# Moving two sums of the second half of a seven-product tile behind the first bank's reads

## The chip, the cores and the metric

The kernel runs on one core of one Trainium2 chip. The time is that of one execution on the device in microseconds (us). The kernel before takes 839.22 us, the median of three runs (838.73 to 839.88). The profile shows one further execution.

## The reference

The input x holds 8 batches of 3008 rows of 256 values. A mixing layer works along the rows, and a layer of two matrix products with a squared ReLU follows:

```
X  = rfft(x, axis=1)                     # per batch, along the 3008 rows
Yr = X.real @ w_r - X.imag @ w_i + b_r   # 256 x 256
Yi = X.real @ w_i + X.imag @ w_r + b_i
Yr, Yi = soft threshold of both at 0.01
y  = irfft(Yr + 1j*Yi, n=3008, axis=1)   # 24064 rows of 256 in all

h   = y @ w_in                           # 256 -> 2048
r   = max(h, 0)
g   = s * r*r + b                        # s and b are scalars
out = g @ w_out                          # 2048 -> 256
```

## The kernel before, in words

**The Fourier layer** is done as small matrix products with constant tables (94 times 32 points). In the steady part it is cut into units (the functions `s1_units`, `s23_units` and `s4_units`), each of a few matmuls into one PSUM bank of the pool `psf` (two banks) and an evacuation by ScalarE (ACT, L187) or VectorE (DVE, L189). Intermediate results go through DRAM (`ud`, `vd`) and come back by transfers on SP's queue, such as `us<-ud` (L644, 384 KB each, four a batch).

**The two matrix products** run over tiles of up to 512 rows. The main loop (L1134 to L1146) takes tile `ti` through 16 slots. In each slot it issues the units of the Fourier layer that the plan puts there, then one sixteenth of the first product of tile `ti` (`first_mm`: two matmuls of 512 columns into `psh`), then one sixteenth of the second product of tile `ti - 1`. After each second slot ACT takes the ReLU out of `psh` (L871, `rt`), and the square into `gt` is taken by ACT (L881) or by DVE (L884). Which one is decided while the program is written down: the function `work` adds an assumed cost to an engine's load, and `act_first` compares the two loads at that point. So an operation that stands elsewhere in the program moves other squares and evacuations between ACT and DVE.

**Seven products instead of eight.** For 21 tiles of 480 or 512 rows (`seven`, L1073: among the last two tiles ahead of each batch's first tile, the first tile of batches 1 and 3 to 6, and those of the last batch but its end) the second product is taken as a 2 by 2 block product with seven block multiplications, n = 0 to 6 in `seven_mms`. The activations of a tile have four blocks a11, a12, a21, a22, each in two halves q = 0 and q = 1 (hidden units 0 to 1023 and 1024 to 2047). `s_op(ti, n, q)` makes the sums that the products need:

- sum 1: s1 = a21 + a22, on DVE, read by product 3
- sum 3: a21 = a11 - a21, on DVE, read by product 5
- sum 2: a11 = a11 - s1, on DVE, after sums 1 and 3 and after product 0 has read a11; read by product 4
- sum 4: a12 = a12 + a11, an accumulating DMA on POOL's queue (L973), after sum 2 and after product 1 has read a12; read by product 6

The products share PSUM banks: {0, 1}, {2}, {3, 4} and {5, 6}. Outside the last batch these banks come from the pool `psa`, which has two buffers. So product 3 opens its bank only when the bank of products 0 and 1 has been read. The reads are `leave(group)`: group 0 reads products 0 and 1 on DVE (L1028 into `zz`, L1029 into `ost`; both run through the helper's line L1012), followed by L1030, which needs no bank. Groups 1, 2 and 3 read the other banks. In the last batch (`alone`) the banks come from both pools, there is no Fourier work left, and product 2 is taken together with products 0 and 1.

The 112 matmuls of the seven products are spread seven to a slot (L1059). In a slot the sums come after its matmuls, and then the reads. The framework then schedules the program: each engine has one queue, in which an instruction that waits holds up all behind it, and the order within a queue can differ from that of the program text, so that a sum, a square and a read may change places. `tc.issue_after(x)` binds the instructions of its block to stand behind x on x's engine.

Of the kernel before, what the change touches and what calls it, by code (L numbers as in the profile page):

```python
# [11 lines left out]
ALU = mybir.AluOpType  # L12
# [84 lines left out]
def kernel(  # L97
# [13 lines left out]
    nc = tc.nc  # L111
    B, S, D = x.shape
# [4 lines left out]
    MC = DFF // P  # L117
# [3 lines left out]
    first, fwd, inv, last = _tables(N)  # L121
# [50 lines left out]
    def matmul(out, lhs, rhs, **how):  # L172
        if pe["on"]:
            pe["now"] += 0.0025 + int(np.prod(rhs.shape[1:])) / 2400.0
        return nc.tensor.matmul(out, lhs, rhs, **how)  # L175

    def work(engine, us):
        load[engine] = max(load[engine], pe["now"]) + us
# [32 lines left out]
    def sum_bank(ti):  # L211
        return any_bank() if ti >= mark[B - 1] // MC else other_bank()
# [149 lines left out]
    b_21 = cpool.tile([P, P], F32, name="b_21")  # L362
# [3 lines left out]
    def w_block(k, j):  # L366
        return w_out_t.rearrange("p (q k) d -> p q k d", k=2)[:, :, k, j * P : (j + 1) * P]
# [447 lines left out]
    def sub_size(tl):  # L815
        return 4 * tl[3] if tl[0] == "wide" else P
# [69 lines left out]
    def store(tl, sub, src):  # L886
        kind, b, j, w = tl
        if kind == "wide":
            h, lo = j
            n2 = HW * h + 4 * sub  # L890
            rows = out[b * N : (b + 1) * N, :].rearrange("(n1 n2) d -> n2 n1 d", n2=N2)
            nc.sync.dma_start(
                out=rows[n2 : n2 + 4, lo : lo + w], in_=src[0 : 4 * w]
            )
            return
        if kind == "main":
            rows = out[b * N + 512 * j : b * N + 512 * (j + 1), :]
            rows = rows.rearrange("(n1 n2) d -> n2 n1 d", n2=N2)[8 * sub : 8 * sub + 8]
            nc.sync.dma_start(out=rows, in_=src)
            return  # L900
        i0 = j + 128 * sub
        end = min(i0 + 128, j + w)
        i = i0
        while i < end:
            hb, r = divmod(i, N2 * 14)
            n2, n1 = divmod(r, 14)
            bt = 2 * b + hb
            rows = out[bt * N + 80 * N2 : (bt + 1) * N, :].rearrange(
                "(n1 n2) d -> n2 n1 d", n2=N2
            )  # L910
            room = min(end, (hb + 1) * N2 * 14) - i
            if n1 == 0 and room >= 14:
                m = room // 14
                cnt = 14 * m
                dst = rows[n2 : n2 + m]
            else:
                cnt = min(14 - n1, room)
                dst = rows[n2, n1 : n1 + cnt]
            nc.sync.dma_start(out=dst, in_=src[i - i0 : i - i0 + cnt])
            i += cnt  # L920
# [40 lines left out]
    def part(ti, q, i, k):  # L961
        size = 2 * sub_size(tiles[ti])
        return gts[(ti, q)][:, i, k, :, 0:size]

    def s_op(ti, n, q):

        size = 2 * sub_size(tiles[ti])
        if n == 1:
            sums[(ti, q)] = spool.tile([P, 4, 2 * P], F16, name="s1", tag="s1")
        s1 = sums[(ti, q)][:, :, 0:size]  # L970
        a11, a12, a21, a22 = (part(ti, q, i, k) for i in range(2) for k in range(2))
        if n == 4:
            nc.gpsimd.dma_start(out=a12, in_=a11, accum_op=ALU.add)  # L973
            return
        out, a, b, op = {
            1: (s1, a21, a22, ALU.add),
            3: (a21, a11, a21, ALU.subtract),
            2: (a11, a11, s1, ALU.subtract),
        }[n]
        nc.vector.tensor_tensor(out=out, in0=a, in1=b, op=op)  # L980
        work("dve", 0.07 + size / 480.0)

    def seven_mms(ti):

        tl = tiles[ti]
        size = sub_size(tl)
        hold = {}
        left = [(0, 0), (0, 1), (1, 1), None, (0, 0), (1, 0), (0, 1)]
        firsts = (0, 2, 3, 5)
        T = T_s[0]  # L990
        right = [w_block(0, 0), w_block(1, 0), T[:, 3], T[:, 0], T[:, 1], T[:, 2], w_block(1, 1)]

        def mm(n, j, c):

            if n in firsts and j == 0 and c == 0:
                hold["ps"] = sum_bank(ti).rearrange("p (n j e) -> p n j e", n=2, j=2)
            if j == 0 and c == 0:
                hold[n] = hold["ps"][0:size, 0 if n in firsts else 1]
            q, g = divmod(c, 4)
            at = slice(j * size, (j + 1) * size)  # L1000
            if left[n] is None:
                lhs = sums[(ti, q)][:, g, at]
            else:
                lhs = gts[(ti, q)][:, left[n][0], left[n][1], g, at]
            matmul(
                hold[n][:, j], lhs, right[n][:, c],
                start=(n in firsts and j == 0 and c == 0), stop=(c == MC // 2 - 1),
                skip_group_check=True,
            )

        def add(out, of, other):
            nc.vector.scalar_tensor_tensor(  # L1012
                out=out, in0=of, scalar=s_bc[0:size], in1=other, op0=ALU.mult, op1=ALU.add
            )
            work("dve", 0.4)

        def wide(t):
            return t[0:size, 0:P].unsqueeze(1).to_broadcast([size, 2, P])

        def leave(group):  # L1020
            if group == 0:
                hold["z"] = zpool.tile([P, 2, 2, P], F32, name="zz", tag="zz")
            if group in (0, 3):
                hold["o", group] = opool.tile([P, 2, D], F32, name="ost", tag="ost")
            z = hold["z"][0:size]
            top = hold["o", 0][0:size]
            if group == 0:
                add(z[:, 0], hold[0], wide(bias_bc))  # L1028
                add(top[:, :, 0:P], hold[1], z[:, 0])  # L1029
                nc.vector.tensor_tensor(out=z[:, 1], in0=z[:, 0], in1=wide(b_21), op=ALU.add)  # L1030
                work("dve", 0.34)
            elif group == 1:
                add(z[:, 0], hold[2], z[:, 0])
            elif group == 2:
                add(z[:, 1], hold[3], z[:, 1])
                two = hold[4].rearrange("p j e -> p (j e)").unsqueeze(1).to_broadcast([size, 2, D])
                zs = z.rearrange("p h j e -> p h (j e)")
                add(zs, two, zs)
                work("dve", 0.27)
            else:  # L1040
                for h in range(2):
                    add(hold["o", 3][0:size, :, h * P : (h + 1) * P], hold[5], z[:, h])
                add(top[:, :, P:D], hold[6], z[:, 1])
                for i in range(2):
                    for j in range(2):
                        store(tl, 2 * (1 - i) + j, hold["o", 3 * (1 - i)][:, j, :])

        C = MC // 2
        alone = ti >= mark[B - 1] // MC
        early = 3 if alone else 2  # L1050
        order = [
            (n, j, c) for h in range(2) for n in range(early) for j in range(2)
            for c in range(4 * h, 4 * h + 4)
        ]
        order += [(n, j, c) for n in range(early, 6) for j in range(2) for c in range(C)]
        order += [(6, j, c) for h in range(2) for j in range(2) for c in range(4 * h, 4 * h + 4)]
        slots = [[] for _ in range(MC)]
        for at, what in enumerate(order):
            slots[at // 7].append(lambda w=what: mm(*w))  # L1059
        first = ((0, 1, 0), (1, 3, 0)) if late(ti) else ()  # L1060
        for at, n, q in (
            *first, (2, 2, 0), (2, 1, 1), (2, 4, 0), (3, 3, 1), (4, 2, 1), (5, 4, 1)
        ):
            at += alone and at > 3
            slots[at].append(lambda n=n, q=q: s_op(ti, n, q))
        for at, group in ((4 + alone, 0), (6, 1), (11, 2), (15, 3)):
            slots[at].append(lambda group=group: leave(group))
        return slots

    def late(ti):  # L1070
        return any(ti == mark[b] // MC for b in range(3, B - 1))
# [29 lines left out]
    mark = {}  # L1101
# [76 lines left out]
```

## Time and profile before

| what | value |
|---|---|
| median of three runs | 839.22 us |
| the profiled execution, its own time | 839.64 us |
| its span, first to last instruction | 837.9 us |
| granted TensorE clock, mean | 0.996 |
| PE (matmul) busy | 822.6 us, 98% |
| DVE busy | 706.9 us, 84% |
| ACT busy | 723.0 us, 86% |
| POOL busy | 86.2 us, 10% |

Some 1.7 us of the profiled execution lie outside its span, and it is 0.4 us above the median. PE's busy time is that of pipelined matmuls whose ends are modelled, so 98% says that matmuls follow one another nearly without a hole, and not that each hole is small: what PE loses shows as gaps between the starts of matmuls and in the list of waits.

### The profile page before, as it was taken

To read this page: it belongs to the slowest core of one execution; us is meant where nothing else is said; L and a number is where in the kernel's file an instruction comes from. 1 tells how busy PE (TensorE), PEld (TensorE's weight loads), DVE (VectorE), ACT (ScalarE), POOL (GpSimd) and SP (SyncE) were. 2 spreads that over 40 slices of the span, in tenths; PEclk is the share of its full clock that TensorE was granted. 3 is DMA by queue.
4 is the path that set the end of the run, shared out by engine and by line. 5 is a ranking of instruction groups with operands and counts; after the bars stand their busy time and mean duration, and the time that the engine had idled before them with its cause. 6 is when DMAs were issued, how large, how long until landed. Compare 5 with 4: busy or idle time off the path is not lost.

```text
span 837.9 us, 19547 instructions
## 1 busy us (share of the span) xinstructions
PE 822.6 (98%) x7662; PEld 600.7 (72%) x7662; DVE 706.9 (84%) x1104; ACT 723.0 (86%) x962; POOL 86.2 (10%) x114
## 2 busy tenths in 40 slices
PE   8999999999999999999999999999999999999997
PEld 7857767777677767777677676767767777767765
DVE  5888989978898888988889888797889988889885
ACT  4998988998899989998889988989889988788882
POOL 4540001100011001100011000100001000001000
PEclk8999999999999999999999999999999999999999
DMA  8954578345873378444773368723565333513321
GB/s 196 180 153 103 124 189 203 63 94 133 198 185 65 94 184 208 114 104 128 195 185 69 88 147 208 175 63 105 127 178 138 67 100 93 137 45 77 72 65 60
DMA packets 116670, 107.17 MB, mean 128 GB/s; under 512 B 12774, under 2 KB 100842, under 8 KB 115234
## 3 DMA queue, kind: packets, MB, share of 16 engines
q1 hardware_dynamic: 102498, 80.55, 33.6%
q0 software_dynamic: 14080, 25.37, 19.1%
q8 instruction: 60, 0.98, 0.5%
q14 instruction: 32, 0.26, 0.1%
HBM read 53.52 MB, written 46.66 MB: 120 GB/s over the span
## 4 chain that ended last, share of the span: by engine, by line
PE 75%; DVE 12%; ACT 6%; DMA 3%; issue 3%; SPq 0%; POOL 0%; DVEq 0%; POOLq 0%
PE psh L175 31%; PE psa L175 28%; PE psf L175 16%; ACT rt L871 3%; DVE gt L884 2%; DVE gt L980 2%; ACT gt L881 1%; DVE ring L699 1%; PE psm L175 1%; DMA gt<-gt 1%; DVE ost L1012 1%; DMA ring<-ring 1%; DVE s L980 1%; DMA x<-in_x_dram 1%; DVE zz L1012 1%
## 5 line engine op out<-in xcount | busy, mean ns | idle before, releaser
L871 ACT ACTIVATE rt<-psh 128x1024 f32<-128x1024 f32 (+2 forms) x384 | 386.7, 1008 | 57.0 <-PE psh L175 55.1
L175 PEld LDWEIGHTS <-gt 128*128 128x128 f16 (+1 forms) x3696 | 304.8, 101 | 167.7 <-DMA gt<-gt 0.5
L175 PE MATMUL psh<-yt,w_in 128*128 128x512 f16 (+1 forms) x1344 | 397.1, 378 | 0.1
L884 DVE TENSOR_TENSOR gt<-rt 128x1024 f16<-128x1024 f32 (+2 forms) x239 | 286.2, 1202 | 78.6 <-ACT rt L871 77.6
L175 PE MATMUL psa<-w_out_t,gt 128*128 128x256 f16 (+3 forms) x2448 | 310.9, 253 | 0.3 <-DMA gt<-gt 0.3
L175 PEld LDWEIGHTS <-w_in 128*128 128x128 f16 x1536 | 136.5, 98 | 24.4 <-issue 1.7
L881 ACT ACTIVATE gt<-rt 128x1024 f16<-128x1024 f32 (+2 forms) x145 | 150.8, 1040 | 3.4
L175 PE MATMUL psa<-T_s,gt 128*128 128x128 f16 (+1 forms) x944 | 79.4, 219 | 0.0
L973 POOL DMA_DIRECT2D gt<-gt x42 | 38.0, 905 | 316.2 <-PE psh L175 66.3
L187 ACT CAST u<-psf 96x512 f16<-96x512 f32 x96 | 55.6, 581 | 9.3 <-PE psf L175 8.6
L699 DVE TENSOR_TENSOR ring<-psf,s 128x512 f16<-128x512 f32 x84 | 57.7, 686 | 3.5 <-PE psf L175 2.5
L187 ACT CAST v<-psf 128x512 f16<-128x512 f32 x79 | 45.8, 583 | 13.6 <-PE psf L175 13.5
L234 POOL DMA_DIRECT2D x<-in_x_dram x36 | 19.2, 539 | 325.1 <-PE psf L175 324.0
L175 PE MATMUL psh<-tail,w_in 128*128 128x512 f16 (+1 forms) x192 | 52.1, 353 | 0.0
L175 PEld LDWEIGHTS <-xf 128*128 128x128 f16 x504 | 46.6, 98 | 6.6 <-DVE xf L672 1.5
L175 PE MATMUL psf<-W_g,xf 128*128 128x256 f16 x336 | 50.4, 272 | 0.0
L187 ACT CAST yt<-psf 128x470 f16<-128x470 f32 (+2 forms) x84 | 43.3, 534 | 3.4 <-PE psf L175 2.2
L1012 DVE SCALAR_TENSOR_TENSOR ost<-psa,s_bc,zz 128x256 f32<-128x256 f32 (+1 forms) x80 | 35.9, 480 | 9.8 <-PE psa L175 8.2
L187 ACT CAST xf<-psf 128x512 f16<-128x512 f32 x64 | 37.4, 585 | 4.2 <-PE psf L175 3.9
L945 DVE SCALAR_TENSOR_TENSOR ost<-psa,s_bc,bias_bc 128x512 f32<-128x512 f32 (+2 forms) x51 | 37.1, 727 | 3.8 <-PE psa L175 1.4
L175 PE MATMUL psf<-x,A_t 94*96 94x512 f16 x102 | 39.0, 382 | 1.4 <-ACT yt L187 0.3
L175 PE MATMUL psf<-C_t,vs 96*128 96x94 f16 (+1 forms) x484 | 37.9, 205 | 0.0
(118 smaller groups left out, 802.6 us busy)
## 6 DMA issues: line engine op xcount, KB each, us to landing
out_dram<-ost SPq DMA_DIRECT2D x152, 128.0 KB
ud<-u SPq DMA_DIRECT2D x56, 192.0 KB
us<-ud SPq DMA_DIRECT2D x28, 384.0 KB
vd<-v SPq DMA_DIRECT2D x42, 256.0 KB
vs<-vd SPq DMA_DIRECT2D x14, 768.0 KB
x<-in_x_dram POOLq DMA_DIRECT2D x28, 376.0 KB, 6.0
gt<-gt POOLq DMA_DIRECT2D x38, 256.0 KB, 4.4
ring<-ring SPq DMA_DIRECT2D x280, 32.0 KB
```

The source lines that it names most:

```text
L175: return nc.tensor.matmul(out, lhs, rhs, **how)
L187: return None, nc.scalar.copy(out=dst, in_=src)
L234: nc.gpsimd.dma_start(out=t[0:N1, i * w : (i + 1) * w], in_=xv[:, c * XCH * D + i * w : c * XCH * D + (i + 1) * w],)
L699: nc.vector.tensor_tensor(out=ring[0][:, i % 4], in0=ps, in1=hold[i // 2][:, i % 2].unsqueeze(1).to_broadcast([P, 2, D]), op=ALU.add,)
L871: nc.scalar.activation(out=rt[:, :, 0:w], in_=ps[:, :, 0:w], func=AF.Relu)
L881: nc.scalar.activation(out=gt, in_=rr, func=AF.Square)
L884: last_square[0] = nc.vector.tensor_tensor(out=gt, in0=rr, in1=rr, op=ALU.mult)
L945: nc.vector.scalar_tensor_tensor(out=ost[0:size, 0:k], in0=ps[0:size, 0:k], scalar=s_bc[0:size], in1=bias_bc[0:size].unsqueeze(1).to_broad ...
L973: nc.gpsimd.dma_start(out=a12, in_=a11, accum_op=ALU.add)
L980: nc.vector.tensor_tensor(out=out, in0=a, in1=b, op=op)
L1012: nc.vector.scalar_tensor_tensor(out=out, in0=of, scalar=s_bc[0:size], in1=other, op0=ALU.mult, op1=ALU.add)
```

## The change

In `seven_mms`, the reads of group 0 are put at the head of what follows the matmuls of their slot (slot 4, or 5 in the last batch). The sums of half q = 1 move: sum 1 from slot 2 to slot 3, sum 3 from slot 3 to slot 5, sum 2 from slot 4 to slot 5 (one slot later each in the last batch, from slot 4 on). Sums 3 and 2 and the DMA of sum 4 are bound behind L1030, the last instruction of group 0; the bond acts on DVE's queue, so it holds sums 3 and 2. The DMA of sum 4 stays in its slot and still waits for sum 2.

The change also has a branch for a tile that stands three ahead of a batch's first one (`third_last`): there sum 4 of half 1 would be a DVE operation in slot 9. The tiles that take seven products ahead of a batch are the last two, so no tile takes that branch: POOL issues 42 such DMAs before, and 42 stand in the changed program.

```diff
+    def third_last(ti):
+        return any(ti == mark[b] // MC - 3 for b in range(2, B))
+
     def s_op(ti, n, q):
...
-        if n == 4:
+        if n == 4 and not (q == 1 and third_last(ti)):
             nc.gpsimd.dma_start(out=a12, in_=a11, accum_op=ALU.add)
             return
         out, a, b, op = {
             1: (s1, a21, a22, ALU.add),
             3: (a21, a11, a21, ALU.subtract),
             2: (a11, a11, s1, ALU.subtract),
+            4: (a12, a12, a11, ALU.add),
         }[n]
...
             if group == 0:
                 add(z[:, 0], hold[0], wide(bias_bc))
                 add(top[:, :, 0:P], hold[1], z[:, 0])
-                nc.vector.tensor_tensor(out=z[:, 1], in0=z[:, 0], in1=wide(b_21), op=ALU.add)
+                hold["left"] = nc.vector.tensor_tensor(
+                    out=z[:, 1], in0=z[:, 0], in1=wide(b_21), op=ALU.add
+                )
...
+        def sums_behind(n, q, behind):
+            if behind:
+                with tc.issue_after(hold["left"].ins):
+                    s_op(ti, n, q)
+            else:
+                s_op(ti, n, q)
...
+        slots[4 + alone].append(lambda: leave(0))
         first = ((0, 1, 0), (1, 3, 0)) if late(ti) else ()
         for at, n, q in (
-            *first, (2, 2, 0), (2, 1, 1), (2, 4, 0), (3, 3, 1), (4, 2, 1), (5, 4, 1)
+            *first, (2, 2, 0), (2, 4, 0), (3, 1, 1), (5, 3, 1), (5, 2, 1),
+            (9 if third_last(ti) else 5, 4, 1),
         ):
-            at += alone and at > 3
-            slots[at].append(lambda n=n, q=q: s_op(ti, n, q))
-        for at, group in ((4 + alone, 0), (6, 1), (11, 2), (15, 3)):
+            at += alone and 3 < at < 8
+            slots[at].append(lambda n=n, q=q, at=at: sums_behind(n, q, at > 4 + alone))
+        for at, group in ((6, 1), (11, 2), (15, 3)):
             slots[at].append(lambda group=group: leave(group))
```

In the order in which the two built programs stand on their engines, the counts of instructions by engine differ in one respect only: 12 evacuations (9 of `yt`, 3 of `xf`) go from DVE to ACT, and 10 squares go from ACT to DVE.

## The prediction

> **What bounds the kernel now.** I read the page's busy times first, then the waits, then the groups by shape, and last the timeline of single tiles.
>
> ```profile
> PE 822.6 (98%) x7662; PEld 600.7 (72%) x7662; DVE 706.9 (84%) x1104; ACT 723.0 (86%) x962; POOL 86.2 (10%) x114
> ```
>
> PE is the bound, and what it loses outside the start-up is short. The list of waits has what the change aims at:
>
> ```profile
> DVE gt L884 <- ACT rt L871: 77.6, 91, 2.3
> ...
> PE psa L175 <- DVE ost L1012: 4.5, 8, 0.9
> ...
> PEld L175 <- DVE ost L1012: 2.0, 6, 0.4
> ```
>
> The last two rows, 6.5 us, are the first matmul of product 3 waiting until DVE's second read (L1012 `ost`) has emptied the bank of products 0 and 1. By the gaps between matmul starts they lie at 11 of the 17 tiles ahead of the last batch. Seven tiles, called A here, stand first among the last two ahead of a batch (reads begin at 134.9, 237.0, 325.8, 427.8, 529.6, 629.8, 727.7): 0.39, 0.30, 0, 0.19, 0.43, 0.19, 0.44, in all 1.94. The five tiles B (151.0, 253.1, 341.3, 443.5, 645.2) lose nothing. The five C, first tiles of a batch, with the `ring` work beside them (170.0, 360.6, 462.9, 562.3, 664.5), lose 0.73, 0.91, 0.91, 1.07, 0.91, in all 4.5. The four D of the last batch (755.3, 768.0, 780.8, 805.3) have more banks and lose nothing.
>
> One A tile on DVE, ahead of and behind the two reads:
>
> ```profile
> 233.61 0.68 DVE L980 TENSOR_TENSOR s<-gt 128x1024 f16<-128x1024 f16 x1
> 234.21 1.15 DVE L884 TENSOR_TENSOR gt<-rt 128x960 f16<-128x960 f32 x1
> 235.28 0.69 DVE L980 TENSOR_TENSOR gt<-gt 128x1024 f16<-128x1024 f16 x1
> 235.88 0.64 DVE L189 CAST yt<-psf 128x470 f16<-128x470 f32 x1
> 236.44 0.68 DVE L980 TENSOR_TENSOR gt<-gt,s 128x1024 f16<-128x1024 f16 x1
> 237.03 0.48 DVE L1012 SCALAR_TENSOR_TENSOR zz<-psa,s_bc,bias_bc 128x256 f32<-128x256 f32 x1
> 237.55 0.48 DVE L1012 SCALAR_TENSOR_TENSOR ost<-psa,s_bc,zz 128x256 f32<-128x256 f32 x1
> ```
>
> Sums 3 and 2 stand ahead of the reads; back to back each takes 0.60 of the queue. The bank's products had ended at 235.8. So the stall is real, and DVE's queue makes it. Two last lines bear on what waits behind sum 2, the first from the view of the tile `gt`, the second from PE's timeline:
>
> ```profile
> DMA to landing us min/median/max: 3.3/4.5/8.8
> ```
>
> ```profile
> 437.34 0.23 PE L175 MATMUL psa<-w_out_t,gt 128*128 128x128 f16 x1 [0.28 <-DMA gt<-gt]
> ```
>
> The first is of the DMAs of sum 4. The second shows one that was too late already: issued at 428.45, landed 8.8 us later, while the four `us<-ud` loads begun at 427.0 ran. From each landing to product 6's first read of that half the trace leaves, in order: A 1.5, 1.5, 2.6, 0.0, 0.6, 1.6, 4.3; B 3.6 to 5.0; C 0.5, 3.7, 4.0, 2.9, 4.2; D 1.9, 1.6, 0.1, 1.9. From the end of sum 2 to product 4's first read: 3.0 to 4.9 in A, B and C, but 1.6, 2.05, 1.3, 1.6 in D.
>
> **The change part by part.** It adds no operation; I work with the order of the built programs and the durations of this execution. Sum 1 of half 1 leaves slot 2 for slot 3, but on DVE it keeps its place, and its price is nothing: product 3 reads it 1.3 us (in D) or more after its end. Sum 4 of half 0 also keeps its place on POOL. SP's queue has nothing of the moved sums; its stores wait for groups 2 and 3 of the reads, which follow PE.
>
> *Reads first, A.* Sums 3 and 2 leave the place ahead of the reads (1.20). But the planner, finding less load on DVE there, gives it a square that ACT took before (1.22 for 1024 columns, 1.15 for 960, 0.95 for 768), and it stands just ahead of the reads. Where its ReLU is early, as at 237.0 (ready at 235.6, square to 236.8), the reads end 0.27 sooner. Tile by tile: 0.13, 0.27, 0, 0.19, 0.43, 0.19, 0.44: a gain of 1.65.
>
> *Reads first, B.* The same square comes ahead of the reads, but in four of the five its ReLU ends only 0.4 to 0.5 before the old reads' start. At 443.5 the square begins 0.3 before, ends its share of the queue at +0.81, reads end at +1.81, and product 3 wanted its bank at +1.58: a new stall of 0.28. The five: 0.24, 0, 0.18, 0.28, 0.12: a loss of 0.8.
>
> *Reads first, C.* From the first read at 341.3 to that at 360.6 DVE took 19.34, 0.46 of it idle. In the new order three operations of 0.6 fewer lie between (sum 2, an evacuation, a `ring` operation), so 17.1; it begins 0.71 late, and the first read comes 1.55 sooner. One `ring` operation now stands between the two reads, so the second ends 1.15 sooner. But on PE's queue the scheduler has moved product 3's first matmul ahead too: three `W_g` (0.109 each), three `w_in` (0.216) and two `T_t` (0.109) matmuls, 1.2 us, filled the wait before and now stand behind it. PE so comes 1.0 sooner (1.2 less B's new 0.18), and of 0.91 some 0.8 stays. Four such tiles gain 0.13 each, the one at 170.0 all of its 0.73: a gain of 1.25. The ends are 4.5 (all of it) and -1 (DVE no sooner).
>
> *Sum 2 later, and with it the DMA.* On DVE sum 2 now stands behind the two reads, L1030, sum 3 and the read of product 2, which itself waits for PE. At 237.0: square to -0.27, reads to +0.65, L1030 to +0.98, sum 3 to +1.58, L1012 to +1.98, sum 2; it began at -0.60. So 2.6 later; in A the seven delays are 2.2, 2.6, 3.4, 2.6, 2.4, 2.6, 2.4, in B 2.5 to 2.9, in C 1.3 and four times 2.6. Behind sum 2 on DVE wait squares and evacuations with slack, on POOL its DMA, and behind that product 6. POOL's other entries there, the loads of x and the `tail` copy, wait for later work anyway. If each DMA takes as long as it did, A waits delay less margin plus the gain above: 0.8, 1.35, 0.8, 2.8, 2.2, 1.25, 0 (9.2), and the first C 1.25: 10.5 in all; B and the other C are covered. If each takes the median 4.5, all of it is hidden: 0. I take 7, nearer the upper end: the long DMAs (6.2 to 8.8 in A) run beside `us<-ud`, and 2.5 us later those still run. In the stretch after 237.0 the 16 DMA engines' share is 0.98 to 1.02 from 241 to 245.
>
> The Trainium skill ("DMA: Bandwidth & Descriptors", Anatomy of one DMA) prices such a transfer at 2.0 us plus its bytes over 436e3 per us, by that page an estimate of 2.6 us for 256 KB, with which this term would be 0; the trace disagrees, its shortest is 3.3. The same page (Issuing engines are not separate DMA queues) says that transfers issued by several engines share the same 16 DMA engines; the trace agrees, with 8.8 us beside `us<-ud`.
>
> *Sum 2 later in D.* No bank wait is there to save. At 755.3: sum 1 from -2.13, the new square from -1.53, first read at -0.39, a second square (1.14), second read 1.14, L1030 1.54, sum 3 1.87, L1012 2.47, sum 2 2.87 to 3.55; it ended at 0.08. So 3.5 later against a margin of 1.6 to product 4. The four: delays 3.5, 4.0, 3.0, 3.5, stalls 1.9, 1.95, 1.7, 1.9, 7.4 in all, less 0.43 each for two `w_in` matmuls that PE's queue now has ahead of that read: 5.7. Sum 4's DMA follows: delay less PE's new lag (about 1.4) less its margin, 0.2, 0.9, 1.6, 0.2, 2.9 in all. Upper end 8.6. The lower end is 4.0, were the new square (1.14) out of the way in the three tiles that have it. I take 6.5: all of the first part and a quarter of the second, since a stall of PE lets DVE catch up.
>
> *Swapped work.* DVE gains 10 squares (11.5) and loses 9 `yt` and 3 `xf` evacuations (7.8); ACT the reverse (-10.1, +6.8). Over 838 us with both under 87% busy: 0, between -1 and +2.
>
> Sum: -1.65 + 0.8 - 1.25 + 7 + 6.5 + 0 = +11.4. On the profiled execution, 839.6 (span 837.9) becomes 851.0; it stood 0.4 above the median, so 850.6.
>
> **The rivals.**
>
> *The bank waits go and nothing takes their place (faster).* For it: the 6.5 us are real, the DMAs might land clear of the loads, and DVE idles 77.6 us at squares whose ReLU is late, so that it could catch up. It needs all landings at or under 4.5 and sum 2 delayed by less than 1.3 to 2.05 in D, which decides it. 839.2 - 6.4 + 0.8 = 833.6. Against it: D's queue, which no landing helps. The Trainium skill ("Perfetto Trace Analysis", Optimizing Tensor Performance) has matmul groups rotate through banks so that the evacuation of one overlaps the next group's matmuls, which speaks for this rival; the trace agrees on the 6.5 us and no further.
>
> *The DMAs land at the median.* Then only D loses: -1.65 + 0.8 - 1.25 + 6.5 = +4.4, 843.6.
>
> *The DMAs meet the loads worse.* All A landings at the 8.8 of 428.45: six of 6.2 to 8.8 become 8.8, 11 us more, and the seventh, 3.3 now, adds 4: +26, 865.
>
> *It does nothing:* the squares put in fill exactly the place of the sums and sum 2's margins hold. D's margins are against it.
>
> **How the numbers follow.** My forecast has 0.62 (845 to 859, by the bounds of the DMA term and of D), landings at the median 0.19, worse landings 0.08, faster 0.08, no change 0.03. A measurement of this kernel can tell about 0.2%. Slower 0.89, same 0.03, faster 0.08. The range 842 to 859 takes in the median landings (D at its lower end would make them 841.1) and leaves out the faster case, no change and the worse landings.
>
> **What would show it.** Right: waits on `DMA gt<-gt` rise from under 1 us to some 7 or more; in the last batch PE waits for DVE `gt` L984 near product 4; the row of waits for `ost` falls little and moves into C and B. Wrong: no such DMA row, sum 2 ending before product 4 in the last four tiles, or an `ost` row that is gone.

## The result, and the profile after

The changed kernel takes 849.58 us, the median of four runs (848.92 to 852.28); the kernel before, run beside it, 839.01 (838.73 to 839.88). The ratio is 1.013, 95% interval 1.0106 to 1.0154: slower by 10.6 us. The profiled execution of the changed kernel took 852.28 (span 850.5, granted clock 0.998) and is the longest of the four, 2.7 above their median; that of before took 839.64 (0.996). The mean clock, a little lower in the kernel before, doesn't explain the difference.

The busy times of the page, of the changed kernel:

```profile
PE 824.0 (97%) x7662; PEld 598.9 (70%) x7662; DVE 709.0 (83%) x1102; ACT 720.1 (85%) x964; POOL 86.3 (10%) x114
```

No engine has much more to do than before (PE +1.4, DVE +2.1, ACT -2.9 us), over a span that is 12.6 longer. The time is in waits. The rows of the list of waits in which PE or its weight loads (PEld) wait for the seven products' sums and banks (us in total, times, longest):

```profile
PEld L175 <- DMA gt<-gt: 9.1, 8, 1.6
...
PE psa L175 <- DMA gt<-gt: 7.7, 8, 1.5
...
PEld L175 <- DVE ost L1016: 5.9, 10, 1.0
...
PEld L175 <- DVE gt L984: 4.7, 4, 1.4
...
PE psa L175 <- DVE ost L1016: 3.7, 8, 0.8
...
PE psf L175 <- DVE gt L984: 2.9, 4, 0.9
```

The waits for `ost`, at which the change is aimed, are nearly as long as before (6.5 and 5.7 us by the gaps below). Two kinds are new: for the accumulating DMA of sum 4 (`DMA gt<-gt`, under 1 us before) and for sum 2 (`DVE gt L984`, no such row before). A weight load and its matmul wait at the same place (`DMA gt<-gt` has eight waits in either row), so rows of PEld and PE must not be added. The prediction did add 4.5 and 2.0; that its 6.5 is right is shown by the gaps, which make 6.48.

To have one figure for each place, I sum the gaps between the starts of consecutive matmuls, each above the usual for its size (the lowest tenth after a matmul of that many columns), where the excess is over 0.03 us. The time from the first matmul's start to the last's, less all such gaps, is 808.8 to 809.1 us in both kernels and in the eleven runs below, so the gaps hold the whole difference. Those within the first 50 us are the start-up. Behind it, by place:

| gaps behind the start-up, us | before | after |
|---|---|---|
| A, product 3 on its bank | 1.94 | 0.37 |
| B, product 3 on its bank | 0 | 1.47 |
| C, product 3 on its bank | 4.54 | 3.88 |
| A, product 6 on the DMA of sum 4 | 0.44 | 4.45 |
| D, product 4 on sum 2 | 0 | 3.58 |
| D, product 6 on the DMA of sum 4 | 0.14 | 4.59 |
| matmuls on `vs`, behind `yt` evacuations or the load of `vs` | 0.21 | 0.98 |
| all | 12.2 | 24.3 |

Product 4's wait, in the first tile of the last batch, on DVE's timeline and then on PE's (start, us, line, what):

```profile
761.14 0.47 DVE L1016 SCALAR_TENSOR_TENSOR ost<-psf,s_bc,zz 128x256 f32<-128x256 f32 x1
761.53 0.41 DVE L1034 TENSOR_TENSOR zz<-zz,b 128x256 f32<-128x256 f32 x1
761.86 0.68 DVE L984 TENSOR_TENSOR gt<-gt 128x1024 f16<-128x1024 f16 x1
762.47 0.47 DVE L1016 SCALAR_TENSOR_TENSOR zz<-psa,s_bc,zz 128x256 f32<-128x256 f32 x1
762.86 0.68 DVE L984 TENSOR_TENSOR gt<-gt,s 128x1024 f16<-128x1024 f16 x1
```

```profile
761.46 0.39 PE L175 MATMUL psf<-T_s,gt 128*128 128x128 f16 x4
761.69 1.03 PE L175 MATMUL psh<-yt,w_in 128*128 128x512 f16 x4
763.60 0.79 PE L175 MATMUL psf<-T_s,gt 128*128 128x128 f16 x11 [0.88 <-DVE gt L984]
...
768.15 0.23 PE L175 MATMUL psa<-w_out_t,gt 128*128 128x128 f16 x1 [1.08 <-DMA gt<-gt]
```

Sum 2 (762.86) ends at 763.54; PE starts again at 763.60. The DMA of sum 4 waits for that same end: POOL issues it at 764.16, it lands 3.9 us later and holds PE once more at 768.15. One late sum makes two waits. In an A tile the second kind alone is left:

```profile
247.50 0.50 PE L175 MATMUL psa<-w_out_t,gt 128*128 128x128 f16 x6
248.96 0.23 PE L175 MATMUL psa<-w_out_t,gt 128*128 128x128 f16 x1 [0.97 <-DMA gt<-gt]
```

### The profile page after: what moved, and what is told of

Same layout as the page of the kernel before. It is cut to its first block, busy times and chain, and to the rows that moved or that the text cites. A ratio compares the mean times of both kernels' runs of the same rounds, so it can differ in the third digit from the quotient of the medians.

```text
span 850.5 us, 19543 instructions
## 1 busy us (share of the span) xinstructions
PE 824.0 (97%) x7662; PEld 598.9 (70%) x7662; DVE 709.0 (83%) x1102; ACT 720.1 (85%) x964; POOL 86.3 (10%) x114
## 5 line engine op out<-in xcount | busy, mean ns | idle before, releaser
L884 DVE TENSOR_TENSOR gt<-rt 128x1024 f16<-128x1024 f32 (+2 forms) x249 | 297.6, 1199 | 79.4 <-ACT rt L871 78.3
L881 ACT ACTIVATE gt<-rt 128x1024 f16<-128x1024 f32 (+2 forms) x135 | 141.0, 1044 | 2.8
L187 ACT CAST yt<-psf 128x470 f16<-128x470 f32 (+2 forms) x93 | 49.1, 541 | 6.2 <-PE psf L175 4.4
L187 ACT CAST xf<-psf 128x512 f16<-128x512 f32 x67 | 39.2, 586 | 3.8 <-PE psf L175 3.6
```

What stands on the lines that cost most here:

```text
L187: return None, nc.scalar.copy(out=dst, in_=src)
L881: nc.scalar.activation(out=gt, in_=rr, func=AF.Square)
L884: last_square[0] = nc.vector.tensor_tensor(out=gt, in0=rr, in1=rr, op=ALU.mult)
```

## The experiments

The theory under test, numbered 1 in the expectations: DVE's queue is what decides, and an operation put behind the reads is paid for where its own reader waits, so that the changed kernel loses in two separate places, the last batch (sum 2, then its DMA) and the A tiles (the DMA), while C gains little because PE's order moved with the reads. The rivals are that the planner's swap of squares and evacuations is the whole loss, that the last batch is all of it, and that the bond is.

In the edits `kind_of(ti)` gives a tile's class A, B, C or D as the prediction names them, and `new_order(ti)` says whether the tile has the order of the changed kernel; where it is false, the reads of group 0 also stand behind the sums again and the bond is off. The edits are shown against the changed kernel. Its lines stand a little lower in them: sums at L994, the DMA at L986, reads at L1026 (L1027 in one kernel). Each time is a median beside runs of the kernel before on the same chip, whose medians there were 839.62 (first four runs), 839.37 (next four) and 839.88 (last three).

### The change everywhere but in the last batch, and only there

```diff
+    def new_order(ti):
+        return kind_of(ti) in 'ABC'     # the other kernel: 'D'
...
+        sums_1 = ((2, 2, 0), (2, 4, 0), (3, 1, 1), (5, 3, 1), (5, 2, 1), (5, 4, 1))
+        if not new_order(ti):
+            sums_1 = ((2, 2, 0), (2, 1, 1), (2, 4, 0), (3, 3, 1), (4, 2, 1), (5, 4, 1))
```

> The change everywhere but in the last batch, whose four tiles keep the order of before. Theory 1 (two independent losses, the last batch's late sums and the late DMAs of the A tiles): what the last batch loses in the changed kernel by the gaps between matmul starts, 8.2 us (3.6 before product 4, 4.6 before product 6), goes, and 849.6 becomes about 841.5, still some 2.5 above before; no wait for gt L984 before psf is left, and the four DMA waits of A stay at some 4.5 us. Rival 2 (the squares that the planner hands to DVE cost DVE and ACT time over the whole kernel): little changes, 847 or more. Rival 3 (the last batch is the whole loss, A, B and C gain on balance): 838 or less.

> The counterpart: the change only in the last batch's four tiles, everything ahead as before. Theory 1: 839.0 plus about 8.2 = 847, with the waits before products 4 and 6 in the last batch as in the changed kernel and the bank waits of before (6.5 us) kept. With e1 the two parts should add up to the whole 10.6 within 1 us. Rival 2 (squares over the whole kernel): at most 842. Rival 3 (last batch is the whole loss and more): 850 or more.

Without the last batch: 841.93 (840.12 to 843.92, 12 runs), ratio 1.0027, interval 1.0015 to 1.0039, that is +2.3. The last batch alone: 846.23 (845.97 to 847.98, 5 runs), ratio 1.0083, 1.0065 to 1.0101, +6.6. The two make 8.9 of the 10.6, not within the 1 us that I had asked for, but with intervals of 1 to 1.5 us on each. The waits of the second kernel:

```profile
PE psa L175 <- DVE ost L1026: 4.5, 8, 0.9
...
PE psa L175 <- DMA gt<-gt: 3.7, 4, 1.3
...
PE psf L175 <- DVE gt L994: 2.9, 4, 0.9
```

The `ost` row is that of before to the digit, the `gt L994` row that of the changed kernel: by the gaps 6.50, and 3.59 before product 4 with 4.40 before product 6. The last batch is some two thirds of the loss, but not all of it, and rivals 2 and 3 fall with these two runs in so far as each was to be the whole.

### The classes A, B and C by themselves

```diff
+    def new_order(ti):
+        return kind_of(ti) in 'C'     # the other kernels: 'A' and 'B'
```

> The change only in the five C tiles (first tiles of batches), all others as before. Theory 1 (the reads come sooner, but product 3's first matmul has moved ahead on PE's queue too, so that the two meet again): the five bank waits of C fall from 4.5 us only to about 3.8, A keeps its 1.9, no wait for a DMA of sum 4 is added: 0.7 us below before, 838.3 to 839.4 where before is 839.0. Rival 6 (the reads' own gain is worth the whole wait, and in the changed kernel it was spoilt by the late tiles around it): C's waits near 0, 834.5 to 836.

> The change only in the seven A tiles. Theory 1, from the changed kernel's own gaps in these tiles: bank waits 1.94 to 0.3 (gain 1.6), waits for the DMA of sum 4 plus 4 to 4.5 less the 0.4 of before, yt evacuations now on ACT plus 0.8 of waits before matmuls on vs: some 3 above before, 841 to 843 where before is 839.4, with DMA waits at 3 to 5 of the seven tiles and none elsewhere. Rival 9 (A is about even, the 2.3 of the run without the last batch come from B and C): 840 or less.

> The change only in the five B tiles, which lost nothing before. Theory 1: the square put ahead of the reads makes new bank waits at four of the five, 1.0 to 1.5 us in all, and no DMA wait, since margins there are 3.6 to 5.0 and sum 2 comes 2.5 to 2.9 later: 0.5 to 1.5 above before, 839.9 to 840.9 where before is 839.4; C's waits may shrink by a few tenths as PE comes later. Rival 9: 841.5 or more.

- C alone: 840.10 (838.30 to 842.08, 11 runs), ratio 1.0004, 0.9995 to 1.0014: no change that can be told, and no gain. The bank waits fell by 0.63, to 0.42, 0.83, 0.83, 0.99 and 0.83, as theory 1 had it, but the first C tile now waits 0.84 for its DMA, which I had not expected here. Rival 6 falls.
- A alone: 842.00 (840.69 to 843.62, 7 runs), ratio 1.0028, 1.0017 to 1.0039: +2.1. The bank waits of A fell to 0.35, and its waits for the DMA stand at 3.16 in four tiles (1.23, 1.03, 0.74, 0.16). Rival 9 falls.
- B alone: 840.08 (838.65 to 841.62, 11 runs), ratio 1.0001, 0.9992 to 1.0010. The new bank waits are there, 0.25, 0, 0.38, 0.39, 0.38, but their 1.4 us are not to be seen in the time (+0.2, at the interval's upper end +0.8, where 0.5 to 1.5 was expected). In its profiled execution nothing takes them back: the gaps behind the start-up stand 2.6 above those of before, and only the start-up is shorter, by 1.4. Why the median doesn't show them stays open.

A, B, C and the last batch alone make 2.1 + 0.2 + 0.7 + 6.6 = 9.6 of the 10.6: the parts add up within their intervals. How little a C tile gains is seen on PE's timeline of the one at 360.6, in the kernel before:

```profile
359.51 0.60 PE L175 MATMUL psf<-W_g,xf 128*128 128x256 f16 x4
359.95 0.59 PE L175 MATMUL psh<-yt,w_in 128*128 128x512 f16 x2
360.38 0.38 PE L175 MATMUL psf<-ring,T_t 128*128 128x256 f16 x2
360.60 0.38 PE L175 MATMUL psh<-yt,w_in 128*128 128x512 f16 x1
361.73 0.61 PE L175 MATMUL psa<-T_s,s 128*128 128x128 f16 x8 [0.75 <-DVE ost L1012]
```

The same tile in the changed kernel, where it is read from 362.3 on, DVE first and then PE:

```profile
362.28 0.48 DVE L1016 SCALAR_TENSOR_TENSOR zz<-psa,s_bc,bias_bc 128x256 f32<-128x256 f32 x1
362.67 0.68 DVE L716 TENSOR_TENSOR ring<-ring 128x1024 f16<-128x1024 f16 x1
363.27 0.48 DVE L1016 SCALAR_TENSOR_TENSOR ost<-psa,s_bc,zz 128x256 f32<-128x256 f32 x1
```

```profile
362.54 0.50 PE L175 MATMUL psa<-T_s,gt 128*128 128x128 f16 x6
362.87 0.27 PE L175 MATMUL psf<-W_g,xf 128*128 128x256 f16 x1
363.81 0.23 PE L175 MATMUL psa<-T_s,s 128*128 128x128 f16 x1 [0.66 <-DVE ost L1016]
```

One matmul of `W_g` stands between product 2's six and product 3's first, where before four of `W_g`, three of `w_in` and two of `T_t` did; a `ring` operation stands between the reads. PE comes to the bank sooner and waits for the second read almost as long.

### The planner's account as before

```diff
         nc.vector.tensor_tensor(out=out, in0=a, in1=b, op=op)
-        work("dve", 0.07 + size / 480.0)
+        if not (q == 1 and new_order(ti) and n in (1, 2, 3)):
+            work("dve", 0.07 + size / 480.0)
...
+        if new_order(ti):
+            for at in (2, 3, 4 + alone):
+                slots[at].append(lambda: work("dve", 0.07 + 2 * size / 480.0))
```

> The order of the changed kernel in all tiles, but the planner's load of DVE is charged for sums 1, 3 and 2 of half 1 in the slots where it was charged before, so that it hands out squares and evacuations as before. Theory 1 (order of sums and reads the main cause, the squares put ahead of the reads an aggravation of 1.15 us per tile): the delay of sum 2 falls from some 2.6 to 1.4 in A and from 3.5 to 2.4 in the last batch, so DMA waits of 9.0 us fall to about 4, product 4's 3.6 to about 1, B's new bank wait of 1.5 goes: 842 to 844. Rival 2 (the planner's swap is the whole loss): 839 or less. Rival 4 (planner makes no difference): 849 to 850.

847.71 (845.63 to 848.37, 5 runs), ratio 1.0089, 1.0070 to 1.0108. The time lies between what theory 1 and rival 4 expected, the profile (845.63, the shortest of the five) speaks for theory 1. A second set of runs of the same kernel:

> The same kernel as e3 once more, since its profiled execution (845.6) was the lowest of its five, which reached to 848.4: does the planner's swap of squares account for 2 us of the loss (median 847.7) or for 5 to 7 (the gaps in its profile behind the start-up, 4.75 more than before)? Theory 1 as told for e3 (order of sums and reads the main cause, the squares put ahead an aggravation of some 3 to 5): gaps behind the start-up 4.5 to 6 above those of before, median 844 to 846. Rival 4 (planner makes next to no difference): median 847 to 849, and gaps of 8 or more above before in this profile.

846.15 (845.55 to 853.05, 6 runs), ratio 1.0090, 1.0065 to 1.0114. Its profile has gaps of 8.0 behind the start-up above those of before, as rival 4 wanted; the first had 5.0, and the median lies just above what theory 1 expected. The waits of the first and then of the second execution of this one kernel:

```profile
PE psa L175 <- DMA gt<-gt: 4.0, 8, 1.1
...
PE psa L175 <- DVE ost L1027: 3.1, 5, 0.8
...
PE psf L175 <- DVE gt L994: 1.7, 4, 0.7
```

```profile
PE psa L175 <- DMA gt<-gt: 7.3, 8, 1.3
...
PE psa L175 <- DVE ost L1027: 3.1, 5, 0.8
...
PE psf L175 <- DVE gt L994: 1.7, 4, 0.7
```

In these two, what DVE's queue decides repeats; what a DMA's landing decides does not. The part that repeats shows what the planner's squares add in the changed kernel: the bank waits fall from 5.71 to 3.9 by the gaps (B's 1.47 and A's 0.37 go, C stays), product 4's wait from 3.58 to 2.36, together 3.0. The median of all eleven runs is 846.49, some 6.8 above before against 10.6 for the changed kernel. So the squares are some 3 to 4 us of the loss, and the order itself is the rest. Rival 2 falls; rival 4 does too, by less, and of theory 1's expectation the size was too good by 2 to 4 us.

### Sum 4 without a DMA

```diff
-        if n == 4 and not (q == 1 and third_last(ti)):
+        if n == 4 and q == 0:
             nc.gpsimd.dma_start(out=a12, in_=a11, accum_op=ALU.add)
             return
...
-            (9 if third_last(ti) else 5, 4, 1),
+            (9, 4, 1),
```

> The changed kernel, with sum 4 of half 1 as a DVE operation in slot 9 in all 21 tiles instead of the accumulating DMA; nothing of the computation is left out. Theory 1: product 6 no longer waits for a DMA, so the 9.0 us of those waits go, the last batch's wait of 3.6 before product 4 and the bank waits of 5.7 stay, and DVE has 21 more operations of 0.6 (12.6 us), which come where it has slack: 840 to 843. Rival 5 (the landing isn't what holds PE, the wait for it would be replaced by the next one, or DVE has no slack): 847 or more.

844.97 (844.76 to 846.95, 6 runs), ratio 1.0067, 1.0050 to 1.0085: 5 us better than the changed kernel, 5.4 above before, and 2 above what I expected. Two rows of its waits:

```profile
PE psa L175 <- DVE ost L1026: 5.5, 8, 1.0
...
PE psf L175 <- DVE gt L994: 2.9, 4, 0.9
```

There is no wait for a landing of sum 4 any more (9.0 by the gaps), and product 4's row is untouched. But DVE's 21 added operations are not free: the bank waits rise from 5.71 to 7.16, and 1.06 come new before matmuls on `gt` that wait for a square. So the landings do hold PE, and rival 5 holds in its other half: DVE had less slack at those places than its idle time of the whole span suggests.

### Without the bond

```diff
-            slots[at].append(lambda n=n, q=q, at=at: sums_behind(n, q, at > 4 + alone))
+            slots[at].append(lambda n=n, q=q: sums_behind(n, q, False))
```

> The changed kernel without the bond: same slots, but sums 3 and 2 of half 1 are not held behind the last instruction of group 0, and the order on DVE is the scheduler's. In the built program sum 3 then stands between the two reads in A and B, sum 2 behind L1030 or the read of product 2. Theory 1 (every 0.6 us of queue is paid at the bank or at the DMA): the second read comes 0.6 later in the A and B tiles, so bank waits rise by some 4 to 7 us from 5.7, while the waits for sum 2 and its DMA fall by about as much: 846 to 851, no real gain over the changed kernel. Rival 8 (the bond itself is what costs): 842 or less.

849.51 (847.62 to 851.59, 6 runs), ratio 1.0110, 1.0093 to 1.0127: no difference from the kernel with the bond that can be told. Three of its waits:

```profile
PE psa L175 <- DVE ost L1026: 9.1, 15, 0.8
...
PE psf L175 <- DVE gt L994: 1.9, 2, 0.9
...
PE psa L175 <- DMA gt<-gt: 1.5, 2, 1.0
```

By the gaps, the bank waits double from 5.71 to 11.64, and the waits for sum 2 and its DMA fall from 12.6 to some 4. DVE's timeline doesn't have the order that the expectation gives. Sum 3 stands between the two reads, with sum 2 behind L1030, in only four of the twelve A and B tiles; in three others sum 2 stands between the reads, and in four of the A tiles both sums stand ahead of them, as they do there in the kernel before, and a square as well. All eleven wait for the bank (0.07 to 0.97), and of the twelve only one waits for the DMA (0.12). The last batch has both orders side by side. In two of its tiles sum 2 stands behind L1030, and they wait 1.09 each before product 4 and then 1.12 and 0.75 for the DMA; in the other two it stands ahead of the second read, and they wait for neither. So in A and B a sum ahead of the second read, and the planner's square with it, is paid at the bank; in the last batch sum 2 behind the reads is paid at its own readers. Rival 8 falls.

### Product 3 later on PE, sums and reads as before

```diff
+    def new_order(ti):
+        return False
...
-            slots[at // 7].append(lambda w=what: mm(*w))
+            slot = 9 if kind_of(ti) == 'C' and 48 <= at < 63 else at // 7
+            slots[slot].append(lambda w=what: mm(*w))
```

In the second kernel, the A tiles too:

```diff
-            slot = 9 if kind_of(ti) == 'C' and 48 <= at < 63 else at // 7
+            slot = 9 if kind_of(ti) == 'C' and 48 <= at < 63 else 7 if kind_of(ti) == 'A' and at == 48 else at // 7
```

> Sums and reads in the order of before in every tile. In the five C tiles only, the first 15 matmuls of the seven products that the program text puts from number 48 on (the opening of product 3's bank among them) are issued two slots later, in slot 9, so that PE's queue has other matmuls where it waited for the second read. Theory 1 (the bank wait of C is PE's order as much as DVE's): C's 4.5 us fall to some 1 us or less, nothing else is moved on DVE, and the time is some 3 us below before: 835.5 to 836.5 where before is 839.0. Rival 7 (whatever stands in that place on PE's queue waits as well, as the changed kernel's C tiles suggest, or the products that now come late hold up product 5's bank): no change, 838.5 to 840, or slower.

> As the run before, and in the seven A tiles the first matmul of product 3 is issued one slot later too. Theory 1: A's 1.9 us of bank waits go as well, with no sum later and so no DMA later: some 1 to 2 us below the run before, 834 to 835.5 where before is 839.0. Rival 7: no change against before, or against the run with C alone.

The matmuls moved are all of product 3 but its last. They stood in slots 6 to 8, so only those of slot 7 move by the two slots that the expectation names.

With C alone: 836.98 (835.94 to 841.13, 8 runs), ratio 0.9977, 0.9961 to 0.9992. With A too: 836.02 (835.34 to 839.08, 12 runs), ratio 0.9963, 0.9951 to 0.9975. Both are faster than before, by 2.4 and 3.4 us, a little less than was expected, and rival 7 falls. The waits for the bank in the first of them:

```profile
PEld L175 <- DVE ost L1026: 2.0, 6, 0.4
...
PE psa L175 <- DVE ost L1026: 1.0, 4, 0.3
```

By the gaps, C's 4.54 fell to 1.23 and A kept its 1.94. In the second kernel A's are gone as well, but 1.6 more than before stand ahead of matmuls on `vs` (some 0.4 of it at the load of `vs`), and the two kernels' times overlap: that A's step gives anything is not shown.

## Why the prediction was right, point by point

The forecast of 850.6 stands 1.0 above the median of 849.58, inside the interval of the ratio. Its terms were less exact than their sum: that the errors cancelled is luck. For the profiled execution it said 851.0, and that took 852.28. The gaps below are of that execution.

- **Reads first, A (-1.65):** right, -1.6 by the gaps, and the same where A was changed alone.
- **Reads first, B (+0.8):** right in place and cause, too small: 1.47. The waits go when the planner's account is put back, so the square ahead of the reads makes them. In time they did not show.
- **Reads first, C (-1.25):** right in kind, -0.66 in size. Four of the five tiles gained 0.08 to 0.09 each instead of 0.13. The tile at 170.0 was to lose its whole wait and kept 0.42: there all four `W_g` matmuls, not three, stand behind product 3. That PE's order took the gain back is shown from the other side by the runs with product 3 later: with DVE's order left alone, 3.3 of C's 4.5 us went.
- **The DMA of sum 4 (+7, 0 to 10.5):** right in place, too large: +4.0 in A, and nothing at the first C tile, which waited 0.84 when C was changed alone and 0.25 and 0.39 with the old account. The step that failed is that the landings stay near those of before: three of A's seven landed in 3.4 to 4.5 us, and the tile that was to lose 2.8 lost 0.51, its DMA having landed in 6.3 us instead of 8.8. The page's median of all these DMAs went from 4.4 to 4.0. The upper end has a slip: by the formula given the first C tile comes to 1.5, not 1.25. This term is also the least certain, since two executions of one kernel differed by 3 us in it. By the Trainium skill ("DMA: Bandwidth & Descriptors", Anatomy of one DMA) such a transfer would take an estimated 2.6 us; the shortest in any run here took 3.2.
- **Sum 2 later in D (+6.5):** 8.0 by the gaps, near the upper end of 8.6, and +6.6 in time when changed alone. Its split failed. Before product 4 I had 5.7, and it is 3.58, since PE's queue had two pairs of `w_in` matmuls ahead of that read where I had counted one (four in a row at 761.69). Before product 6 I had a quarter of 2.9, "since a stall of PE lets DVE catch up", and it is 4.59: the DMA is issued only after the end of sum 2, however long PE waits, and what PE doesn't lose at product 4 it loses at product 6. The lower end of 4.0 takes the squares off the 7.4 from which the `w_in` matmuls were not yet taken; with the planner's account as before, D still lost 5.9 and 7.4 in the two profiles.
- **Swapped work (0, between -1 and +2):** +0.8, the waits of 0.27 before matmuls on `vs` in three A tiles. Each is ended by a `yt` evacuation of DVE that stands behind a square, as at 333.59, where the square before it began at 332.45. They stand in the run with A alone as well.

The gaps so make -1.6 + 1.5 - 0.7 + 4.0 + 8.0 + 0.8 = +12.0, against +12.1 counted over all of them and 12.6 between the two profiled executions; 0.5 of the latter is a longer start-up. The medians lie 10.6 apart, so about 2 of these 12.6 us belong to the executions that were profiled. The forecast range of 845 to 859 doesn't follow from the bounds named for it, the DMA term's and D's: they give 841.1 to 856.2.

Of the rivals, the faster one failed at the last batch, as said: its four tiles had no bank wait to lose. "Landing at the median" came true in three A tiles; with no landing at all the kernel still stands 5.4 above before. Worse landings came in none of the seven: the longest of them took 6.5 us, and the longest of all 42 DMAs 7.0.

## What to carry to other kernels

Before moving an operation behind another on an engine's queue, follow it to its own readers: here sums of 0.6 us each, moved from ahead of a read, came back as two waits, one at the sum's reader and one at the DMA that waits for it, and only the tiles with a margin above the delay were free of both. Look at what fills the wait on the waiting engine too: moving PE's own opening of the bank later, with DVE's order untouched, gained 2.4 us where the change to DVE in the same tiles gained nothing. Where a planner balances engines by position, expect it to fill the place that a move sets free.

## What the runs showed of the hardware that was not expected

- Of one kernel, two profiled executions have the same waits for DVE to 0.1 us, but 4.0 and 7.3 us of waits for the accumulating DMAs. Of this kernel, a cost that hangs on a landing needs several executions to be known.
- The start-up differs between executions: the gaps of the first 50 us are 9.5 to 12.6 us over thirteen profiled executions, and it goes with the granted clock. In six profiles the clock of the first 20 us is 1.00, and these start-ups are 9.5 to 9.8. In the other seven it is 0.83 or 0.91, and theirs are 10.3 to 12.6; both kernels' profiles are among the seven. The waits of matmuls for the loads of x differ as well, from 1.6 to 4.5 us.
- The twelve runs of the fastest kernel lie at 835.3 to 836.9 and at 838.2 to 839.1, with nothing between. What makes the two groups was not shown: the mean granted clock lies between 0.996 and 1.000 in both.
